# Attention output turned by 72-column groups and written transposed to DRAM, in a fused attention and MLP block

## The chip, the cores and the metric

The kernel runs on one core of one Trainium2 chip. The metric is the device time of one execution in microseconds, the median of three runs. The core has TensorE (PE, matrix products), VectorE (DVE), ScalarE (ACT), GpSimd (POOL) and the sync engine (SP). The last two issue DMA transfers here, SP plain ones and POOL those that accumulate. Each engine works through its own instructions in order.

## The reference

With x of 2048 tokens by 576 columns, normalised once to xn, the result is x plus an attention branch plus an MLP branch:

```python
def _A_ref(x, wqkv, wo):
    H = 32; Dh = D // H                      # 32 heads of 18 columns
    W, dil = 8, 2                            # 8 keys, every second token back
    q, k, v = split(x @ wqkv)
    idx = pos[:, None] - arange(W)[None, :] * dil
    attn = softmax(where(idx >= 0, q . k[idx] * Dh ** -0.5, -1e9))
    o = sum_w attn[w] * v[idx[w]]
    return o.reshape(B, S, D) @ wo

def _B_ref(x, w1, w2, w3, w4):
    h = gelu(layernorm(x) @ w1)              # four column blocks, then shifted by +1 -1 +2 -2 tokens
    x1 = x + shifted(h) @ w2
    return x1 + gelu(layernorm(x1) @ w3) @ w4    # 576 -> 4608 -> 576

xn = layernorm(x)
return x + _A_ref(xn, A_wqkv, A_wo) + _B_ref(xn, B_w1, B_w2, B_w3, B_w4)
```

Everything is fp32. The kernel multiplies in fp32r: each operand is split into a high and a low part (`split_w`, `signed`), and three of the four part products are summed.

## The kernel before

The work runs in stages, each ordered by hand. First q, k and v are computed and spilled to DRAM in 24 groups of 72 columns, four heads each (`qkvd`); then comes the token mixing with w1 and w2; then the MLP with w3 and w4. The MLP has two halves. For the first 6 pairs of column blocks it works in `units` of 512 tokens (`up`, L1241, and `down`). For the remaining 12 pairs it works in 24 steps, q = 0 to 23, twelve for each half of the tokens, with z = q - 24. One step is seven block products of a scheme that forms sums of operands in place of an eighth product (`product`, L1552, items P1 to P7) and eight down tiles (D0 to D7), in the order of `ORDER` (L1759). What else a step does hangs on these items: `at("D6", load_pair, ...)` places the load of a later pair of w3 blocks (L1382, L1385) after item D6, and so on. The last step, q = 23, is written out token by token in `ORDER_END` together with the output product o @ wo (items `k`, `y`, `c`: L2042, L2055, L2048) and the stores to `out`.

A down tile accumulates in PSUM (`down_mm`, L1288). `down_out` evicts it: into Y by ScalarE (L1300) or VectorE (L1303), or, for the ten tiles of `YD` whose rows live in DRAM, by ScalarE into a staging row (L1297), from which POOL adds it to `yd` by an accumulating DMA (L1298). `staging` (L1219) picks the row. While `EV[0]` is None these are three own rows of the pool `evp` and row 2 of Y in turn.

The attention is a generator (`attention`, L1100) that runs on VectorE beside TensorE's products. `bg` (L1197) is called between items with a budget in microseconds; each `yield` charges the estimated cost of the operation just issued. In a step the budget is 1.5 per item less what the item itself put on VectorE. For each of eight groups of four heads it computes eight pairs of multiply and reduce (w = 0 to 7, the last four as double width: L1162, L1165), a softmax, and in `av` (L1122) the weighted sum of the eight shifted v. A token is `p * 16 + j`: partition p holds 16 consecutive tokens. The result `o_` lies in `po[:, 0]`, 16 x 72 values on each partition, and one DMA writes it to `od`, in token order. The v of the next group is loaded right after. When z = -6 has come to item P4 the generator is run out whatever is left, its memory is given back, and rooms for wo, for the turned rows (`ST`) and for staging are taken from it.

The output product needs o with its columns on the partitions. In the steps z = -5 to -2 each item of a list reads one tile of 128 tokens of `od` in four DMAs (`load_o`, L1749), turns the tile before in blocks of 32 x 32 on VectorE (`o_turn`, L1757), and after every four tiles `put_o` writes the turned block in four DMAs to `on[b]` (576 x 512, L935). The end order then reads `on` into the operands of the output product (`read_x`, L1651, L1655). The loads of wo (`load_wo`, L1604, L1608) are placed in z = -5, those of w4 (L906) after D5 of each step.

Of the kernel before, what the change touches and what calls it, by code (L numbers as in the profile page):

```python
# [17 lines left out]
NT = S // 128  # L18
# [98 lines left out]


ORDER_END = """
xlp P1 cb gA lA D0 E0 P6 A0 P2 k2 P7 tf xr0.0 w40 gB wh24 P5 xr0.1 xr0.2 k3 xr0.3 xr0.4 xo1 xo3 D1  # L120
D2 E1 z3 P3 wt04 xr1.0 xr1.1 E2 A1 A2 D3 wh02 g22 lB E3 A3 D4 E4 D5 xh0.01 A4 D6 P4 wl wl02 wl24
z2 xs0.0 xs0.1 xs0.2 xt0.01 E5 A5 D7 E6 A6 w41 L3 xp1 xt0.13 xh1.01 l22 g12 E7 A7 xr1.2 xl1.01 l12
D8 xr1.3 xr1.4 E8 D9 xh0.13 gC lC rows xs0.3 E9 xt0.35 L2 xh0.57 xt0.57 A8 D10 E10 A9 D11 E11 L1
A10 D12 xl0.13 E12 A11 D13 xh1.13 A12 E13 xt1.01 A13 xt1.13 D14 D15 xo2 xh0.35 xr2.0 xr2.1 xr2.2
xr2.3 xr2.4 E14 E15 A14 xl0.01 xl0.57 A15 out k0.1 c0 k1.1 c1 k0.2 xl0.35 xs1.0 xs1.1 xs1.2 xs1.3
xh1.35 k0.5 k1.5 y0.2 k2.1 c2 xl1.35 xp2 xt1.35 y0.5 k0.6 y0.6 xl1.13 xh1.57 xl1.57 xh2.01 y1.5
xt1.57 k1.6 y1.6 k0.3 y0.3 k0.7 y0.7 k1.2 y1.2 k1.3 y1.3 k1.7 y1.7 xt2.13 L7 xt2.01 xl2.01 xh2.13
k0.4 y0.4 k2.2 k1.4 k3.1 c3 xl2.13 L5 y1.4 xr3.0 xr3.1 xp3 k2.6 y2.2 xs2.0 k2.5 xr3.2 xr3.3 y2.6
xr3.4 xs2.1 xs2.2 xs2.3 xt2.35 k3.6 y3.6 xh2.35 y2.5 k2.7 y2.7 xt2.57 k3.5 y3.5 xl2.35 k4.1 c4
k3.7 L10 y3.7 xh2.57 L15 xl2.57 k2.4 y2.4 xt3.13 o4 k4.2 xh3.13 k3.2 y3.2 xt3.01 L9 xs3.0 k4.6  # L130
y4.6 k4.5 y4.5 xh3.01 xl3.01 k5.1 o2 c5 xs3.1 k4.7 y4.7 L11 xs3.2 k3.4 k4.4 y3.4 k5.2 xh3.35 xs3.3
y4.4 xt3.35 xt3.57 xh3.57 y4.2 o8 y5.2 o3 xl3.13 xl3.57 k6.1 L13 c6 k7.1 c7 k3.3 k5.6 y5.6 y3.3 o5
k2.3 y2.3 o6 k5.7 o7 k5.5 y5.5 k7.6 xl3.35 k6.2 o0 y5.7 k5.3 y7.6 y5.3 k5.4 y5.4 o11 o1 k4.3 y4.3
o10 y6.2 k6.6 y6.6 k6.5 y6.5 k7.2 y7.2 k6.7 y6.7 k7.5 y7.5 k6.3 y6.3 k7.3 o9 o13.0 k7.7 o14 y7.3
y7.7 o15 k6.4 y6.4 k7.4 y7.4 o12 o13.1
"""


# [5 lines left out]
def fused_block(ctx, tc, x, wqkv, wo, w1, w2, w3, w4, out):  # L144
# [36 lines left out]
    TS, XS = KV[0:96, 2:3], KV[0:96, 3:4]  # L181
    ST = None
    qkvd = dram.tile([24, HALO + S, GC], F32, name="qkvd")
    od = dram.tile([S, D], F32, name="od")
    w3t = dram.tile([NWP, 32, 384], F32, name="w3t")
    yd = {t: dram.tile([128, D], F32, name=f"yd{t}") for t in YD}
    xn = [dram.tile([D, 512], F32, name=f"xn{b}") for b in range(NB)]
# [912 lines left out]
    def attention(ap):  # L1100
# [21 lines left out]
        def av(g):  # L1122
            if g == NG - 1:
                exp_now()
            L, v = Ls[g], vs[g]
            o, out = (o_, po[:, 0, :]) if g < NG - 1 else (
                qs[g].rearrange("p j (h d) -> p (j h) d", d=HD), qs[g].rearrange("p j d -> p (j d)"))
            Lf = L.rearrange("p j h w -> p (j h) w")
            dve.tensor_reduce(den[g], Lf, axis=AX.X, op=ALU.add)
            dve.reciprocal(den[g], den[g])  # L1130
            yield 0.8
            dve.tensor_tensor(Lf, Lf, den[g][:, :, None].to_broadcast([128, TPP * GH, W]),
                              op=ALU.mult)
            yield 0.6
            for w in range(W):
                vv = v[:, DIL * w:DIL * w + TPP, :].rearrange("p j (h d) -> p (j h) d", d=HD)
                dst = prod if w else o
                dve.tensor_tensor(dst, vv, Lf[:, :, w:w + 1].to_broadcast([128, TPP * GH, HD]),  # L1138
                                  op=ALU.mult)
                yield 1.35  # L1140
                if w:
                    dve.tensor_tensor(o, o, dst, op=ALU.add)  # L1142
                    yield 1.35
            sp.dma_start(od.rearrange("(p j) d -> p j d", p=128)[:, :, g * GC:(g + 1) * GC],
                         out.rearrange("p (j c) -> p j c", c=GC))

        yield None
        qs[0], ks[0] = load("q", 0, 0, False, pool), load("k", 1, 0, True, pool)
# [2 lines left out]
        for g in range(NG + 1):  # L1151
            if g < NG:
                q, k = qs[g], ks[g]
                L = Ls[g] = ap.tile([128, TPP, GH, W], F32, name="L", bufs=2)
                Lf = L.rearrange("p j h w -> p (j h) w")
                Lw = Lf.rearrange("p x w -> p w x")
                qf = q.rearrange("p j d -> p (j d)")
                for w, n in ((0, 1), (1, 1), (2, 1), (3, 1), (4, 2), (6, 2)):
                    dst = po[:, 2 - n:2, :]
                    win = bass.AP(tensor=k.tensor, offset=k.offset + DIL * w * GC,  # L1160
                                  ap=[list(k.ap[0]), [DIL * GC, n], [1, TPP * GC]])
                    dve.tensor_tensor(dst, qf[:, None, :].to_broadcast([128, n, TPP * GC]), win,  # L1162
                                      op=ALU.mult)
                    yield 0.15 + 1.2 * n
                    dve.tensor_reduce(Lw[:, w:w + n, :],  # L1165
                                      dst.rearrange("p w (x d) -> p w x d", d=HD),
                                      axis=AX.X, op=ALU.add)
                    yield 0.15 + 1.2 * n
                if g + 1 < NG:
                    qs[g + 1], ks[g + 1] = load("q", 0, g + 1, False), load("k", 1, g + 1, True)  # L1170
                mx = den[g] = ap.tile([128, TPP * GH], F32, name="mx", bufs=2)
                dve.tensor_tensor(L, L, mask4, op=ALU.add)
                yield 0.6
                dve.tensor_reduce(mx, Lf, axis=AX.X, op=ALU.max)
                yield 0.6
                dve.tensor_tensor(Lf, Lf, mx[:, :, None].to_broadcast([128, TPP * GH, W]),
                                  op=ALU.subtract)
                yield 0.6
                exp_now()
                state["exp"] = lambda L=L: act.activation(L, L, AF.Exp, scale=float(HD) ** -0.5)  # L1180
                if g == NG - 1:
                    vs[g] = load("k", 2, g, True)
                if g == 0:
                    yield 4.0
            if g:
                yield from av(g - 1)
                if g < NG - 1:
                    vs[g] = load("v", 2, g, True)

    state = {"gen": None, "debt": 0.0, "exp": None, "done": False}  # L1190

# [19 lines left out]
    def temp(t, n=512):  # L1211
        return Y[:, t, :n]
# [6 lines left out]
    def staging():  # L1219
# [1 line left out]
        if EV[0] == "nt":  # L1221
            return ntpool.tile([128, D], F32, name=f"ev{evc[0] % 3}")
        if EV[0] is None:
            n = evc[0] % 4
            return evp.tile([128, D], F32, name=f"ev{n}") if n < 3 else temp(2, D)
        return temp(EV[0][evc[0] % len(EV[0])], D)
    hid = {}

# [353 lines left out]
        for t, parts in prev:  # L1582
            yield lambda t=t, parts=parts: down(t, parts)

    otile = {}
    OF = {"A11": (0, 0), "A12": (0, 1), "A22": (0, 2), "S2": (1, 0), "S3": (1, 1), "S4": (1, 2),
          "S1": (1, 3), "B11": 0, "B21": 1, "B22": 2, "T1": 3, "T3": 4, "T2": 5, "T4": 6}
    WF, XF = {}, {}
# [152 lines left out]
            return f["tail"][0:96, i, :]  # L1741
        return f["hi"][:, v - 3, i, :] if v > 2 else f["lo"][:, v - 1, i, :]

    def load_o(t):
        b, i = divmod(t, 4)
        otile[t] = temp(9 + t % 3, D)
        for q in range(4):
            r = 512 * b + 128 * q + 32 * i
            sp.dma_start(otile[t][32 * q:32 * q + 32], od[r:r + 32, :])  # L1749

    def put_o(b):
        for q in range(4):
            n_put(b, q, on)

    def o_turn(t):
        c = t % 4 * 32
        dve.transpose(ST[:, :, c:c + 32], otile[t].rearrange("p (j c) -> p j c", c=32))  # L1757

    ORDER = "P1 D0 P2 P6 D1 P5 D2 P7 D3 P4 D4 P3 D5 D6 D7"  # L1759
    ORDERS = {0: "P1 P2 D0 P6 P5 P7 D1 D2 P4 P3 D3",  # L1760
              NWP - 1: "P1 D0 P2 P6 P5 P7 D1 P4 P3 D2 D3 D4 D5 D6 D7",
# [2 lines left out]
    for q in range(NQ):  # L1764
# [93 lines left out]
                at("D6", load_pair, q + 2 + (q == NWP - 2))  # L1858
        else:
            break  # L1860
        if -5 <= z <= -2:
            for i, (it, nx) in enumerate((("P6", "P6"), ("D1", "D1"), ("P5", "P5"), ("P4", "P4"))):
                t = 4 * (z + 5) + i
                at(it, o_turn, t)
                if t + 3 < NT:
                    at(nx, load_o, t + 3)

        if z < -1 and q + 1 != NWP:
            at("D5" if q else "D3", load_w4, NPL + pair(q + 1), 0)
        if 0 < q < 9:  # L1870
            at("D6", sums, 1, q - 1)
        if 0 < q - sb * NWP <= 5:
            at("D7", load_xa, YD[5 - 5 * sb + q - sb * NWP - 1])
        if -5 <= z < -1:
            at("P4", put_o, z + 5)
        if z == -2:
            at("D7", load_w4, NPL + pair(q + 1), 1)
        if z == -5:
# [10 lines left out]
        for it in ORDERS.get(q, ORDER).split():  # L1889
# [39 lines left out]
                tiles[int(it[1])]()  # L1929
            for f in plan.get(it, ()):  # L1930
                f()
            if (z < -6 or z == -6 and EV[0]) and (q, it) != (NWP, "P6"):
                bg(1.5 - spent[0], it == "P6" and q != NWP - 1 or (q, it) == (NWP, "P3"))
                spent[0] = 0.0
                if (z, it) == (-6, "P4"):
                    while not state["done"]:
                        bg(1e9)
                    apc.__exit__(None, None, None)
                    wop = tc.tile_pool(name="wop", bufs=1, reuse_waits="tile")
                    wopool = wop.__enter__()  # L1940
                    room_wa()
                    opc = tc.tile_pool(name="op", bufs=1, reuse_waits="tile")
                    room(opc.__enter__())
                    evc_pool = tc.tile_pool(name="evp", bufs=1, reuse_waits="tile")
                    evp = evc_pool.__enter__()
                    EV[0] = None
                    for t in range(3):
                        load_o(t)
    END, last = {}, {}
    q, g = NQ - 1, NQ - 2  # L1950

# [3 lines left out]
    def open_last():  # L1955
        nonlocal xlp, xlpool
        evc_pool.__exit__(None, None, None)
        opc.__exit__(None, None, None)
        EV[0] = (9, 11, 10, 2)
        xlp = tc.tile_pool(name="xlp", bufs=1, reuse_waits="tile")  # L1960
        xlpool = xlp.__enter__()
# [167 lines left out]
```

## Time and profile before

| what | us |
|---|---|
| median of three runs | 1261.26 |
| lowest and highest run | 1258.53, 1264.15 |
| the profiled execution | 1262.52 |
| its span, first to last instruction | 1260.7 |
| TensorE, VectorE, ScalarE, GpSimd busy | 1237.5, 959.4, 776.4, 298.6 |

The mean granted clock of TensorE is 0.995 of full speed. In the profile's rows an engine's busy time and the number of its instructions stand together; "PEld" is TensorE's loading of stationary operands, which overlaps its products. A chain row gives its start, its length and what ran. A wait row names who waited for what: the total, the number of times, the longest. A group row ends with the idle time just before its instructions and what ended it. Lines marked L are those of the kernel printed above.

### The profile page before, as it was taken

To read this page: it belongs to the slowest core of one execution; us is meant where nothing else is said; L and a number is where in the kernel's file an instruction comes from. 1 tells how busy PE (TensorE), PEld (TensorE's weight loads), DVE (VectorE), ACT (ScalarE), POOL (GpSimd) and SP (SyncE) were. 2 spreads that over 40 slices of the span, in tenths; PEclk is the share of its full clock that TensorE was granted. 3 is DMA by queue.
4 is the path that set the end of the run, shared out by engine and by line. 5 is a ranking of instruction groups with operands and counts; after the bars stand their busy time and mean duration, and the time that the engine had idled before them with its cause. 6 is when DMAs were issued, how large, how long until landed. Compare 5 with 4: busy or idle time off the path is not lost.

```text
span 1260.7 us, 20054 instructions
## 1 busy us (share of the span) xinstructions
PE 1237.5 (98%) x7305; PEld 1137.3 (90%) x7305; DVE 959.4 (76%) x1244; ACT 776.4 (62%) x1264; POOL 298.6 (24%) x436
## 2 busy tenths in 40 slices
PE   9999999999999999999999999999999999998798
PEld 8999988999898999999899998999899999887798
DVE  8877546698388989996678898999999865354486
ACT  4555566356455545547778678676768667575661
POOL 4523000031321121112123223222222222221230
PEclk9999999999999999999999999999999999899899
DMA  8879795168888695868688987989866878998885
GB/s 234 203 182 222 161 245 166 38 178 230 225 195 201 159 193 114 197 150 222 126 189 178 214 205 154 212 177 243 188 151 120 186 148 196 211 195 173 181 214 186
DMA packets 221627, 231.97 MB, mean 184 GB/s; under 512 B 100072, under 2 KB 157800, under 8 KB 221400
## 3 DMA queue, kind: packets, MB, share of 16 engines
q1 hardware_dynamic: 187864, 162.72, 46.3%
q0 software_dynamic: 33664, 67.97, 33.4%
q8 instruction: 57, 0.93, 0.3%
q14 instruction: 42, 0.34, 0.1%
HBM read 131.58 MB, written 108.30 MB: 190 GB/s over the span
## 4 chain that ended last, share of the span: by engine, by line
PE 63%; DMA 5%; ACT 2%; DVE 2%; issue 1%; SPq 0%; ACTq 0%; DVEq 0%
PE ps L1288 31%; PE cc L1558 18%; PE p L1252 10%; DMA w3st<-in_B_w_dram 3%; PE ca L2042 2%; PE cc L2042 1%; DMA Y<-in_B_w_dram 1%; PE cb L2042 1%; DMA yd<-Y 1%; DVE w3st L1393 0%; DMA xt<-xn 0%; DVE xt L954 0%; ACT Y L1297 0%; ACT ev L1297 0%; SPq L1382 0%
## 5 line engine op out<-in xcount | busy, mean ns | idle before, releaser
L1288 PEld LDWEIGHTS ps<-w,c 128*128 128x128 f32 x3456 | 481.3, 190 | 26.7 <-ACT ev L1297 6.4
L1288 PE MATMUL ps<-w,c 128*128 128x288 f32 x3456 | 491.7, 298 | 10.1 <-ACT ev L1297 5.3
L1298 POOL DMA_DIRECT2D yd<-Y x159 | 144.3, 910 | 373.5 <-ACT Y L1297 318.2
L1243 DVE TENSOR_TENSOR c<-Y,c 128x512 fp32r<-128x512 f32 x144 | 98.6, 685 | 87.8 <-ACT Y L1232 83.0
L1297 ACT COPY Y<-ps 128x576 f32<-128x576 f32 x159 | 100.9, 635 | 72.0 <-PE ps L1288 59.8
L1558 PE MATMUL cc<-xt,w3s 128*128 128x512 f32 (+1 forms) x504 | 129.2, 397 | 6.6 <-DVE Y L1568 6.0
L1558 PEld LDWEIGHTS cc<-xt,w3s 128*128 128x128 f32 (+1 forms) x504 | 93.2, 190 | 24.9 <-DVE Y L1568 6.5
L1300 ACT COPY Y<-ps 128x576 f32<-128x576 f32 x89 | 56.9, 639 | 52.3 <-PE ps L1288 51.0
L1162 DVE TENSOR_TENSOR po<-q,k 128x1152 f32<-128x1152 f32 (+1 forms) x48 | 84.2, 1754 | 0.8
L1558 PE MATMUL cc<-xB,w3a 128*128 128x512 f32 (+1 forms) x336 | 84.7, 392 | 0.0
L1165 DVE TENSOR_REDUCE L<-po 128x64 f32<-128x1152 f32 (+1 forms) x48 | 84.0, 1751 | 0.8
L1231 ACT ACTIVATE c<-p 128x512 fp32r<-128x512 f32 x48 | 28.7, 598 | 88.7 <-PE p L1252 88.7
L1138 DVE TENSOR_TENSOR po<-v,L 128x1152 f32<-128x1152 f32 x56 | 75.4, 1354 | 0.9
L1558 PEld LDWEIGHTS cc<-xB,w3a 128*128 128x128 f32 (+1 forms) x336 | 60.5, 188 | 10.0
L436 PE MATMUL p<-wb,xt 128*128 128x432 f32 (+1 forms) x336 | 68.3, 362 | 0.2 <-ACT wb L325 0.2
L1142 DVE TENSOR_TENSOR po<-po 128x1152 f32<-128x1152 f32 x49 | 66.4, 1355 | 0.9
L436 PEld LDWEIGHTS p<-wb,xt 128*128 128x128 f32 (+1 forms) x336 | 62.5, 189 | 3.3 <-ACT wb L325 0.6
L1568 DVE TENSOR_TENSOR Y<-cc,Y 128x512 f32<-128x512 f32 x49 | 33.5, 684 | 39.1 <-ACT Y L1564 34.6
L200 POOL TENSOR_TENSOR rs<-rs,mhalf 128x1 f32<-128x1 f32 x32 | 22.6, 707 | 163.5 <-DVE mv L203 93.6
L1269 ACT COPY ps<-Y 128x576 f32<-128x576 f32 x89 | 57.5, 646 | 3.1 <-DVE Y L1303 1.2
L708 PE MATMUL ca<-wb,xt 128*128 128x432 f32 (+1 forms) x280 | 58.5, 360 | 0.0
L708 PEld LDWEIGHTS ca<-wb,xt 128*128 128x128 f32 (+1 forms) x280 | 52.6, 189 | 2.8 <-ACT keep L715 0.4
(349 smaller groups left out, 2244.0 us busy)
## 6 DMA issues: line engine op xcount, KB each, us to landing
yd<-Y POOLq DMA_DIRECT2D x161, 288.0 KB, 6.0
Y<-in_B_w_dram SPq DMA_DIRECT2D x29, 576.0 KB, 6.0
w3st<-in_B_w_dram SPq DMA_DIRECT2D x56, 256.0 KB, 8.4
qkvd<-stg SPq DMA_DIRECT2D x44, 216.0 KB, 3.3
yd<-ev POOLq DMA_DIRECT2D x21, 288.0 KB, 7.7
w3st<-in_B_w_dram SPq DMA_DIRECT2D x92, 64.0 KB, 7.6
Y<-in_A_x_dram SPq DMA_DIRECT2D x16, 288.0 KB, 4.2
xn<-st SPq DMA_DIRECT2D x16, 288.0 KB, 4.4
```

Source lines behind the costliest of these rows:

```text
L436: pe.matmul(ps[:, :QB], xo[:n, o + k, a, :], W[:n, w + k, v, :], start=i == 0, stop=i == len(PLAIN) - 1)
L708: pe.matmul(ps, form(g // 2, x, n, a), W[:n, OP[w], v, :], start=start and i == 0, stop=stop and i == len(HALVES) - 1, skip_group_check=True)
L1138: dve.tensor_tensor(dst, vv, Lf[:, :, w:w + 1].to_broadcast([128, TPP * GH, HD]), op=ALU.mult)
L1142: dve.tensor_tensor(o, o, dst, op=ALU.add)
L1162: dve.tensor_tensor(dst, qf[:, None, :].to_broadcast([128, n, TPP * GC]), win, op=ALU.mult)
L1165: dve.tensor_reduce(Lw[:, w:w + n, :], dst.rearrange("p w (x d) -> p w x d", d=HD), axis=AX.X, op=ALU.add)
L1243: dve.tensor_tensor(h[:, 1, :], g, h[:, 0, :].bitcast(F32), op=ALU.subtract)
L1252: pe.matmul(ps, W3[f][:, w, :], x1n[b][:, a, :], start=n == 0, stop=n == len(PAIRS) - 1)
L1288: pe.matmul(ps[:, k, :HF], h[:, col], w[:, p, k * HF:(k + 1) * HF], start=n == 0 and not seed, stop=n == len(seq) - 1, skip_group_check=True)
L1297: act.copy(e.rearrange("p (h c) -> p h c", h=2), ps[:, :, :HF])
L1298: pool.dma_start(yd[t], e, accum_op=ALU.add)
L1558: pe.matmul(ps, WX[w][:k, v, SLOT[w], :], area[sb][xk][:k, a, :], start=onto is None and i == 0, stop=last and i == len(HALVES) - 1, skip_ ...
```

## The change

`od` and the functions `load_o`, `o_turn` and `put_o` go, with the calls that placed them in z = -5 to -2. In place of the one write to `od`, `av` turns the group itself, in three windows of 32 columns that start 24 columns apart, into the memory of the group's v. Block b of 32 partitions then holds 24 columns of the window for 512 tokens, which are the tokens of `on[b]`; four DMAs of 24 rows write them. The last group uses `po` like the others.

```diff
-            o, out = (o_, po[:, 0, :]) if g < NG - 1 else (
-                qs[g].rearrange("p j (h d) -> p (j h) d", d=HD), qs[g].rearrange("p j d -> p (j d)"))
+            o = o_
...
-            sp.dma_start(od.rearrange("(p j) d -> p j d", p=128)[:, :, g * GC:(g + 1) * GC],
-                         out.rearrange("p (j c) -> p j c", c=GC))
+            turned = v.rearrange("p j c -> p (j c)")[:, :3 * 512].rearrange("p (b x) -> p b x", b=3)
+            for b in range(3):
+                win = bass.AP(tensor=po.tensor, offset=po.offset + 24 * b,
+                              ap=[list(po.ap[0]), [GC, TPP], [1, 32]])
+                dve.transpose(turned[:, b, :].rearrange("p (c j) -> p j c", j=TPP), win)
+                yield 0.7
+            for b in range(NB):
+                sp.dma_start(dram_ap(on[b], g * GC * 512, [[512, 24], [24 * 512, 3], [1, 512]]),
+                             turned[32 * b:32 * b + 24])
```

The load of v moves from the end of `av` into the pairs of the next group, after the third:

```diff
                     yield 0.15 + 1.2 * n
+                    if w == 2 and g > 1:
+                        vs[g - 1] = load("v", 2, g - 1, True)
...
                 yield from av(g - 1)
-                if g < NG - 1:
-                    vs[g] = load("v", 2, g, True)
```

The attention may run up to item D2 of z = -5 instead of P4 of z = -6; its memory is given back there, without a room for turned rows. Staging has five own rows in place of three and Y[2]:

```diff
-            n = evc[0] % 4
-            return evp.tile([128, D], F32, name=f"ev{n}") if n < 3 else temp(2, D)
+            return evp.tile([128, D], F32, name=f"ev{evc[0] % 5}")
...
-            if (z < -6 or z == -6 and EV[0]) and (q, it) != (NWP, "P6"):
-                bg(1.5 - spent[0], it == "P6" and q != NWP - 1 or (q, it) == (NWP, "P3"))
+            if (z < -5 or z == -5 and EV[0]) and (q, it) != (NWP, "P6"):
+                bg(1.5 - spent[0], it == "P6" and q != NWP - 1)
                 spent[0] = 0.0
-                if (z, it) == (-6, "P4"):
+                if (z, it) == (-5, "D2"):
```

`ORDER_END` holds nearly the same items in another order. Its first lines, before and after:

```diff
-xlp P1 cb gA lA D0 E0 P6 A0 P2 k2 P7 tf xr0.0 w40 gB wh24 P5 xr0.1 xr0.2 k3 xr0.3 xr0.4 xo1 xo3 D1
-D2 E1 z3 P3 wt04 xr1.0 xr1.1 E2 A1 A2 D3 wh02 g22 lB E3 A3 D4 E4 D5 xh0.01 A4 D6 P4 wl wl02 wl24
+xlp gA lA P1 cb D0 D1 E0 E1 P2 P6 w40 A0 A1 D2 k2 P7 wh02 P5 xo1 D3 tf k3 z3 xr0.0 w41 xr0.1 P3
+wh24 xr0.2 xr0.3 xr0.4 E2 xr1.0 xr1.1 g22 A2 wt04 l22 D4 E3 E4 A3 A4 xt0.01 D5 E5 z2 g12 D6 A5 D7
...
```

In it P, D and E are products, down tiles and their evictions, A opens the next bank, `w40` and `w41` split the last w4, `xr` reads `on`, `xh`, `xt`, `xl` and `xs` form the operands from it, and `wh`, `wt`, `wl` those from wo.

## What the change should do to the time

> **What bounds the kernel now.** I read the page first, then the busy time by stage, the chain of work that ended last, the sync engine's timeline, and what VectorE waited for.
>
> ```profile
> span 1260.7 us, 20054 instructions
> PE 1237.5 (98%) x7305; PEld 1137.3 (90%) x7305; DVE 959.4 (76%) x1244; ACT 776.4 (62%) x1264; POOL 298.6 (24%) x436
> ```
>
> TensorE is busy for all but 23.2 us, so an edit that takes nothing from TensorE can only win back idle or slowed TensorE time. Where that time lies is read by stage. One step of the second MLP half (seven products, eight down tiles) is one window below; I call the steps q0 to q23. The first window is a step in mid-run, the next four are q19 to q22 from first product to first product, then q23 with its downs (the written-out end order), then the output products.
>
> ```profile
> core 0: us, PE busy (x) PEld busy (x) DVE busy (x) ACT busy (x) POOL busy (x), PEclk, DMA share, GB/s
> 1003.50:1027.50 24.00, 24.00 (x147) 21.97 (x146) 22.33 (x23) 16.80 (x28) 7.05 (x9) 1.00 0.73 135
> 1048.40:1072.40 24.00, 24.00 (x146) 21.98 (x146) 12.44 (x17) 16.80 (x27) 5.99 (x8) 1.00 0.98 233
> 1072.40:1102.20 29.80, 26.90 (x146) 24.53 (x146) 12.02 (x17) 16.83 (x27) 6.10 (x8) 0.89 0.91 213
> 1102.20:1129.20 27.00, 24.58 (x146) 21.86 (x146) 12.17 (x18) 18.06 (x29) 7.09 (x9) 1.00 0.91 194
> 1129.20:1157.20 28.00, 24.78 (x146) 21.74 (x145) 16.13 (x23) 16.79 (x29) 5.99 (x7) 1.00 0.84 176
> 1157.20:1204.80 47.60, 40.32 (x244) 37.08 (x243) 20.11 (x28) 29.63 (x46) 13.90 (x17) 0.93 0.88 183
> 1204.80:1257.00 52.20, 52.17 (x393) 51.93 (x391) 43.44 (x91) 19.06 (x34) 9.75 (x13) 1.00 0.73 204
> ```
>
> A step at full pace takes 24.0 us. q20, q21 and q22 take 29.8, 27.0 and 28.0: 5.8 + 3.0 + 4.0 = 12.8 us lost. The chain has the price of one product and of three downs:
>
> ```profile
> 1067.60 4.79 PE ps L1288 x36
> 1072.39 1.61 PE cc L1558 x7
> ...
> 1081.29 11.22 DMA w3st<-in_B_w_dram
> ...
> 1092.59 0.60 ACT w3a L1398
> ...
> 1093.93 0.53 ACT ev L1297
> ...
> 1094.51 7.68 PE ps L1288 x36
> ...
> 1111.96 8.56 DMA w3st<-in_B_w_dram
> ...
> 1137.53 11.12 DMA w3st<-in_B_w_dram
> ...
> 1157.49 14.81 DMA Y<-in_B_w_dram
> ```
>
> So q23 with seven products and sixteen downs needs 7 x 1.61 + 16 x 1.60 = 36.9 us and took 47.6: 10.7 lost. The output products lose nothing (52.17 busy of 52.2). All told 12.8 + 10.7 = 23.5 us are lost after 1072, and next to nothing before. The chain also says how: a load of w3 (`w3st`) arrives late, ScalarE's cast L1398 waits for it, the eviction L1297 stands behind that cast in ScalarE's order, and TensorE waits for the bank. In q23 it is the load of w4 into Y.
>
> Why do these loads come late? The sync engine issues them in program order:
>
> ```profile
> 1024.51 1.02 SPq L1382 DMA_DIRECT2D w3st<-in_B_w_dram  x2
> ...
> 1080.36 1.47 SPq L1382 DMA_DIRECT2D w3st<-in_B_w_dram  x2
> ...
> 1109.61 3.03 SPq L1382 DMA_DIRECT2D w3st<-in_B_w_dram  x2
> ...
> 1134.76 4.80 SPq L1382 DMA_DIRECT2D w3st<-in_B_w_dram  x2
> ```
>
> In mid-run the issue falls at the first product of the step (1024.4). In q20, q21, q22 it falls 8.0, 7.4 and 5.5 us after it (1072.4, 1102.2, 1129.2). What stands ahead on that queue, and on VectorE, is the late work on o:
>
> ```profile
> SPq L1749 <- DMA yd<-Y: 9.1, 2, 6.5
> SPq L1749 <- DMA od<-q: 7.5, 1, 7.5
> ...
> L1757 DVE STREAM_TRANSPOSE st<-Y 128x576 f32<-128x576 f32 x16 | 11.9, 763 | 27.6 <-DMA Y<-in_B_w_dram 9.7 <-DMA on<-st 8.5 <-DMA wr<-in_A_wo_dram 7.7
> ...
> Y<-od SPq DMA_DIRECT2D x64, 72.0 KB, 3.2
> on<-st SPq DMA_DIRECT2D x16, 288.0 KB, 8.1
> ```
>
> 64 reads and 16 writes stand in one queue with the weight loads, each with waits of its own; the sixteen turns held VectorE idle for 27.6 us; and the DMA share is 0.98, 0.91 and 0.91 where mid-run has 0.73.
>
> **The change, part by part.**
>
> *The late reads, turns and writes go.* 64 x 72 KB and 16 x 288 KB are 9.2 MB, with their SP issues and 16 x 0.763 = 12 us of VectorE. With the queue clear, the w3 issue goes back to the start of the step. In mid-run a w3 load has from 1024.4 to its cast 13.3 us into a step (q19: cast at 1061.72, step from 1048.40):
>
> ```profile
> 1061.72 0.84 ACT L1398 CAST w3a<-w3st 128x768 fp32r<-128x768 f32 x1
> w3st<-in_B_w_dram SPq DMA_DIRECT2D x56, 256.0 KB, 8.4
> ```
>
> 8.4 us to landing leaves some 4 us of slack, and even the 11.2 us of q20 would fit. I take back 12.3 of the 12.8 us of q20 to q22; 0.5 stays for the six loads of wo, which remain in q19.
>
> *The end.* In q23 the w4 load was issued at 1157.49, because VectorE's previous w4 split was late behind the turns, and it took 14.81 us among the last writes of o, the first reads of them, and accumulates.
>
> ```profile
> 1176.76 3.36 PE L1558 MATMUL cc<-xt,w3s 128*128 128x512 f32 x7 [5.72 <-DVE Y L1568]
> 1180.12 7.45 PE ps L1288 x48
> ```
>
> This cost TensorE 5.72 us of idle, then a product of 3.36 us for 1.61 and four downs of 7.45 for 6.39 (the clock granted is 0.93 in this window): 5.7 + 1.8 + 1.1 = 8.6 us. Mid-run issues the same load ahead of the step's first product, so I count it gone. The other 2.1 stays, and I charge 2.1 more because q23 compressed to 37 us must still read the new forms' inputs (0.88 x 47.6 = 42 us of DMA work in the window, of which the writes of o, 1.2 of 183 GB/s x 47.6 us = 8.7 MB, go). Net gain at the end: 6.5 us. The end order is rearranged, with the same kinds of work; by itself I cost that at nothing, below 2 us either way. Two output rows stand last on the queue as before.
>
> *The turns move into the attention.* 24 of 128x512 instead of 16 of 128x576: by elements 512/576 x 763 = 0.68 us each, 16.3 us in all. They lie beside TensorE's products, paid from the attention's budget of VectorE time, as the 0.7 in the code says. What is unproven is their write, whose elements lie 64 bytes apart; all rows of transposes here write runs of 32. From below: 0.68 us, nothing lost. From above the dearest element that VectorE shows is the reciprocal's, 553/64 = 8.6 ns, so 4.4 us a turn.
>
> ```profile
> L1130 DVE RECIPROCAL mx<-mx 128x64 f32<-128x64 f32 x8 | 4.4, 553 | 0.3
> 420.00:567.00 147.00, 147.00 (x874) 133.93 (x873) 139.89 (x122) 75.52 (x123) 25.15 (x29) 1.00 0.74 153
> 640.00:960.00 320.00, 319.22 (x1922) 291.35 (x1921) 288.47 (x305) 233.16 (x366) 86.27 (x101) 1.00 0.85 191
> ```
>
> VectorE has 7.1 us free from 420 to 567 (three groups, nine turns) and 31.5 from 640 to 960 (the five other groups, fifteen turns). I take 0.7 us, the nearest row being the same instruction. The Trainium skill, "SBUF — State Buffer", section "Door 1: The DMA port swizzle", speaks against it: accesses that leave a 16-byte line pay a penalty, and here every written element does. It gives no size, and no run here shows one; at twice the time, an estimate, the sum stays, because the extra still fits the free time above.
>
> *The attention ends later.* Its last stretch:
>
> ```profile
> 984.25 0.68 DVE L1129 TENSOR_REDUCE mx<-L 128x64 f32<-128x512 f32 x1
> L1142 DVE TENSOR_TENSOR q<-q,po x7: 1347/1354/1360, 989.5 to 1025.0; 128x1152 f32<-128x1152 f32 x7
> ```
>
> By the yields in the code these 42 us held 21.65 us of budget, 0.51 a us. The 24 x 0.7 = 16.8 more take 33 us: the end moves from 1026 to 1059, just where the new closing point lies (q19, before its third down: 1048.4 + 6 x 1.6 = 1058 to 1060). VectorE had 11.6 us free in q19 (12.44 busy of 24). At most a few operations are forced there; cost 0, and up to 10 us if I am wrong (a rival).
>
> *The stores.* Per group four DMAs of 24 rows in runs of 2 KB replace one with runs of 288 bytes, the same 590 KB with the padding left out. The v load moves behind the third pair of the next group and waits for them. In a tight group that place and the start of the weighting are
>
> ```profile
> 512.00 1.36 DVE L1162 TENSOR_TENSOR po<-q,k 128x1152 f32<-128x1152 f32 x1
> 529.78 0.68 DVE L1129 TENSOR_REDUCE mx<-L 128x64 f32<-128x512 f32 x1
> v<-qkvd SPq DMA_DIRECT2D x6, 576.0 KB, 9.3
> ```
>
> 18 us for 9.3, cost 0, with at most 3 us per group if SP is held. On SP, weight loads would stand behind that wait; 4 us of slack covers it.
>
> *Staging.* Five own rows replace three and Y[2] in q19 to q22. Evictions wait less for a free row, never longer: nothing on the low side, and on the high side only what these steps lose, which the 12.3 already counts. I add 0.
>
> **Sum.** 12.3 + 6.5 = 18.8 us: span 1241.9. The profiled execution took 1262.52 us, 1.8 more than its span; the median of the runs is 1261.26, so the time is 1261.26 - 18.8 = 1242.5.
>
> **Rivals.**
> 1. *The end stays bound by its loads.* For it: a DMA share of 0.88 there and ScalarE's in-order casts. Against: 1.2 MB of writes less and w4 issued earlier. q20 to q22 alone give 12.3: 1249.0.
> 2. *The attention closes late* and a burst of forced VectorE work, followed by wo loads waiting for its memory on SP, holds q19 and q20. For it: a 33 us estimate that lands on the closing point. Against: free VectorE time. It gives back 10 us: 1252.5.
> 3. *Nothing moves.* The loads are late because DMA is full, not because of SP's order. For it: 0.98 share in q19. Against: q19 lost nothing at that share. About 1260.
> 4. *Slower: the turns' scattered writes.* At a price t per turn, 24 x (t - 0.7) less the 38.6 us free falls on TensorE through VectorE's order; it eats the gain from t = 3.1 us, four and a half times the plain turn. At 4.4 us it costs 50 us: 1292. Against: strided operands elsewhere (the products with L) run at the plain rate. The skill's rule above is this rival's ground, without a size.
>
> **How the numbers follow.** Forecast 0.60, rival 1 0.23, rival 2 0.07, rival 3 0.06, rival 4 0.04. This kernel's measurement can tell about 0.5%, 6.3 us, from no change. Faster: 0.60 + 0.23 + 0.06 of rival 2 = 0.89; same: 0.01 + 0.06 = 0.07; slower: 0.04. The range runs from all 23.5 us won back (1237.8, rounded to 1237.0) to rival 2 (1253.0).
>
> **What would show it.** Right: windows of 24.0 us for q20 to q22; the w3 issue at the first product; no wait for a w3 or w4 load ahead of an eviction; transposes of 0.7 us at eight places between 440 and 1060; the output products starting near 1186. Wrong: transposes over 1.4 us; products waiting for VectorE between 420 and 570; a stall in q19 or q20 behind the wo loads; TensorE idle by more than 4 us in q23.

## The result, and the profile after

| | before | after |
|---|---|---|
| median of the runs, us | 1262.68 | 1242.37 |
| lowest and highest run, us | 1258.53, 1264.15 | 1240.77, 1245.73 |
| the profiled execution, us | 1262.52 | 1240.77 |
| its span, us | 1260.7 | 1239.0 |

The ratio is 0.9848, with an interval of 0.9815 to 0.9881. (Before was run once more beside after, which moves its median from 1261.26 to 1262.68.) The profiled execution of after is the fastest of its four, so the spans differ by 21.7 us and the medians by 20.3. The first lines of the page after:

```profile
span 1239.0 us, 19946 instructions
PE 1230.8 (99%) x7305; PEld 1133.3 (91%) x7305; DVE 972.0 (78%) x1252; ACT 776.5 (63%) x1264; POOL 299.4 (24%) x436
```

TensorE has the same 7305 products in 6.7 us less busy time, and its idle time went from 23.2 to 8.2 us. 6.7 + 15.0 = 21.7: two thirds of the gain are waits that went, one third is products that had run slowly in the windows that held those waits.

The windows by stage of after: q19 to q22 and then the start of the end order, each cut at 24 us, so that kernels can be compared line by line. "PEclk" is the last column but two, then come DMA share and GB/s.

```profile
core 0: us, PE busy (x) PEld busy (x) DVE busy (x) ACT busy (x) POOL busy (x), PEclk, DMA share, GB/s
1048.00:1072.00 24.00, 24.00 (x147) 21.97 (x146) 16.60 (x20) 16.80 (x28) 6.00 (x8) 1.00 0.86 201
1072.00:1096.00 24.00, 24.00 (x147) 21.96 (x146) 9.66 (x13) 16.80 (x28) 5.98 (x8) 1.00 0.74 153
1096.00:1120.00 24.00, 24.00 (x147) 21.97 (x146) 11.32 (x15) 19.31 (x32) 7.65 (x10) 1.00 0.66 125
1120.00:1144.00 24.00, 24.00 (x147) 21.97 (x146) 13.30 (x17) 16.79 (x28) 5.92 (x8) 1.00 0.64 126
1144.00:1183.00 39.00, 38.90 (x257) 36.63 (x256) 22.12 (x32) 30.02 (x47) 15.15 (x18) 1.00 0.99 207
```

TensorE is busy for all but 0.1 us, at full clock. In the experiments I use two measures. One is the number of products in the last four windows: 147 + 147 + 147 + 257 = 698 here. The other is the delay of a product: e1, with the old end order, apart, the kernels derived from after run the same products in the same order, so I take the product that after starts at 1183, how much later another kernel starts it, and subtract the same delay at 1048. That gives the microseconds lost in between.

The sync engine's timeline of after, in q19 and later (start, length, queue, line, tile, number of DMAs):

```profile
1057.67 3.34 SPq L1149 DMA_DIRECT2D on<-k  x4
1064.02 1.16 SPq L1607 DMA_DIRECT2D wr<-in_A_wo_dram  x2
1069.39 0.37 SPq L905 DMA_DIRECT2D Y<-in_B_w_dram  x1
...
1074.47 0.99 SPq L1386 DMA_DIRECT2D w3st<-in_B_w_dram  x2
...
1098.24 0.90 SPq L1386 DMA_DIRECT2D w3st<-in_B_w_dram  x2
...
1120.15 0.99 SPq L1386 DMA_DIRECT2D w3st<-in_B_w_dram  x2
...
1142.08 0.38 SPq L905 DMA_DIRECT2D Y<-in_B_w_dram  x1
```

The w3 loads of q20, q21 and q22 are issued within 2.5 us of the first product of their step, where before it was 8.0, 7.4 and 5.5. The w4 load is issued at 1142.08, 2 us ahead of q23; before it was 1157.49, at q23's first product. The first store of the last group stands at 1057.67: the attention ends there.

The first output product of after, the only output product that waits, and the turns of the first seven groups (timeline and groups; the bracket is the idle time before it and who ended it):

```profile
1181.21 0.29 PE L2016 MATMUL cc<-wfs,xfh 128*128 128x288 f32 x1
1206.05 0.40 PE L2016 MATMUL cc<-wfs,c 96*128 96x288 f32 x1 [1.55 <-DMA c<-wr]
...
L1146 DVE STREAM_TRANSPOSE v<-po 128x512 f32<-128x512 f32 x21 | 21.0, 1064 | 0.2
```

q23 starts at 1144.2, so it takes 37.0 us, the full-pace price. A turn takes 1.06 us. The turn of 576 columns in before takes 0.763, which scales to 0.68 for 512.

### The profile page after: what moved, and what is told of

The parts are those of the page before. It is cut to its first block, busy times and chain, and to the rows that moved or that the text cites. A ratio compares the mean times of both kernels' runs of the same rounds, so it can differ in the third digit from the quotient of the medians.

```text
span 1239.0 us, 19946 instructions
## 1 busy us (share of the span) xinstructions
PE 1230.8 (99%) x7305; PEld 1133.3 (91%) x7305; DVE 972.0 (78%) x1252; ACT 776.5 (63%) x1264; POOL 299.4 (24%) x436
## 4 chain that ended last, share of the span: by engine, by line
PE 64%; DMA 3%; DVE 2%; ACT 2%; issue 2%; SPq 0%; DVEq 0%; ACTq 0%; POOLq 0%
PE ps L1292 32%; PE cc L1562 20%; PE p L1256 10%; DMA w3st<-in_B_w_dram 1%; PE ca L2016 1%; DMA c<-on 1%; PE cc L2016 1%; DMA c<-wr 1%; DMA w3a<-wr 0%; DVE wr L1674 0%; DVE w3st L1397 0%; PE cb L2016 0%; DVE w L915 0%; DVE po L1167 0%; DVE w3s L1408 0%
## 5 line engine op out<-in xcount | busy, mean ns | idle before, releaser
L1140 DVE TENSOR_TENSOR po<-po 128x1152 f32<-128x1152 f32 x56 | 75.9, 1355 | 1.0
```

## The experiments

Four reasons stood against each other. **Q**: the late work on o holds the queues of SP and VectorE, and the weight loads behind it come late. **B**: its bytes fill the DMA engines. **O**: the new end order does a good part. **W**: it takes the writes to do the damage. Each kernel ran four to ten times. Small losses are read from the windows and not from medians, because the stretch before q19 varies from profile to profile: among e1, e3 to e6, e9 and e10, which do not touch it, the product that after starts at 1048 comes from 0.9 us earlier to 4.2 us later.

**1. The end order alone.** After with the old `ORDER_END`, and before with the new one:

```diff
 # after, e1_old_end_order             # before, e2_new_end_order_before
-    ORDER_END = """xlp gA lA P1 ...    -    ORDER_END = """xlp P1 cb gA ...
+    ORDER_END = """xlp P1 cb gA ...    +    ORDER_END = """xlp gA lA P1 ...
```

> The changed kernel with the end order of before, nothing else. Theory Q (the late reads, turns and writes of o held SP's order, VectorE's order and the DMA engines, and so made the weight loads late): q20 to q22 stay at 24.0 us each and q23 takes 37 to 41 us, time 1240 to 1248. Rival O (the rearranged end order won q23's 10.7 us): q23 takes 45 us or more, time 1250 to 1254.

> The kernel before with the new end order, nothing else. Theory Q: q20 to q22 lose 12 to 13 us as before, q23 still takes 44 us or more, time 1257 to 1264. Rival O: q20 to q22 lose 12 to 13 us, q23 takes 37 to 40, time 1250 to 1254.

1242.32 us (ratio to before 0.9841, 0.9821 to 0.9860) and 1267.45 us (1.0032, 1.0017 to 1.0047). e1 loses nothing in q20 to q22. Its last window, in the columns used above:

```profile
1144.00:1183.00 39.00, 38.08 (x251) 35.80 (x250) 19.10 (x27) 29.54 (x47) 13.98 (x17) 1.00 0.91 196
```

The chain of work of e2:

```profile
1079.93 11.46 DMA w3st<-in_B_w_dram
...
1155.07 15.76 DMA Y<-in_B_w_dram
```

The old order runs 251 products in the last window where the new one runs 257, about a microsecond, and gives it back by the end. With the late work in place the new order wins nothing: the same loads are late. e2's median is even 4.4 us above that of before run beside it (1263.02), clear of the noise and above my range of 1257 to 1264. Its profiled execution, the fastest of its ten, has a span within 0.2 us of before's and does not show where these 4 us go; that stays open. O falls.

**2. The late work, one kind at a time.** Into after I put back, in z = -5 to -2 and at the old places, work that nothing uses: the reads (52 DMAs of 72 KB from `on` into free rows of Y), or the writes (16 DMAs of 288 KB, in runs of 512 bytes, to a spare tensor).

```diff
+    def late_read(t):                                   # e3_late_reads
+        b, i = divmod(t, 4)
+        for q in range(4):
+            sp.dma_start(temp(9 + t % 3, D)[32 * q:32 * q + 32],
+                         dram_ap(on[b], 128 * 512 * q + 18432 * i, [[D, 32], [1, D]]))
```
```diff
+    def late_write(b):                                  # e4_late_writes
+        for q in range(4):
+            src = temp(9, D)[32 * q:32 * q + 32]
...
+            sp.dma_start(dram_ap(late[b], 128 * q, [[512, 32], [32 * 512, 18], [1, 128]]), blk)
...
+        if -5 <= z < -1:
+            at("P4", late_write, z + 5)
```

> The changed kernel with 52 reads of 72 KB from the finished o into the free rows 9 to 11 of Y put back in q19 to q22, at the places of before, with nobody using what they read; no turns, no writes. Theory Q, in the form that the waits behind the turns did the harm: 0 to 3 us lost in q20 to q22, time 1242 to 1246. Rival B (the bytes alone, whoever waits): 3.7 of the 8.5 MB, so 4 to 9 us lost, time 1246 to 1252.

> The changed kernel with 16 writes of 288 KB in runs of 512 bytes to a spare tensor put back after P4 of q19 to q22; no reads, no turns. Theory Q, in the form that the waits behind the turns did the harm: 0 to 3 us lost in q20 to q22, time 1242 to 1246. Rival B: 4.7 of the 8.5 MB in the shortest runs, so 5 to 9 us lost, time 1247 to 1252.

1244.92 us (0.9865, 0.9837 to 0.9892) and 1244.54 us (0.9857, 0.9838 to 0.9876). The window of e3 with the highest DMA share:

```profile
1072.00:1096.00 24.00, 24.00 (x147) 21.96 (x146) 9.64 (x14) 16.79 (x28) 6.01 (x7) 1.00 1.03 253
```

Step windows of e4:

```profile
1072.00:1096.00 24.00, 24.00 (x147) 21.94 (x145) 7.66 (x13) 15.12 (x25) 5.04 (x6) 1.00 0.99 233
1096.00:1120.00 24.00, 23.23 (x139) 20.97 (x138) 11.61 (x16) 19.85 (x33) 7.60 (x9) 1.00 0.98 206
```

DMA engines busy for the whole window (1.03, 0.99, 0.98), and TensorE loses nothing to the reads and 0.9 us to the writes. A full DMA share is no sign of a loss by itself: B, as a matter of the share, falls.

**3. Two and three kinds together.** e5 adds turns to the reads, e6 all three, e9 reads and writes without turns, e10 turns and writes without reads. These have a room `ST` for the turned rows and before's staging (three own rows and Y[2]).

```diff
+    def late_turn(t):
+        c = t % 4 * 32
+        dve.transpose(ST[:, :, c:c + 32], temp(9 + t % 3, D).rearrange("p (j c) -> p j c", c=32))
...
+        if -5 <= z <= -2:
+            for i, (it, nx) in enumerate((("P6", "P6"), ("D1", "D1"), ("P5", "P5"), ("P4", "P4"))):
...
+                at(it, late_turn, t)                    # e5, e6, e10
...
+                    at(nx, late_read, t + 3)            # e5, e6, e9
...
+            at("P4", late_write, z + 5)                 # e6, e9, e10
```

> The changed kernel with 52 late reads of 72 KB and 13 late turns of what they read, at the places of before (from the last item but four of q19 on), into a spare block; staging of three own rows and Y[2]; no late writes. A read must now wait on SP until VectorE has turned the row it overwrites, and VectorE's queue waits for the read. Theory Q: the ring of waits between SP and VectorE is what makes the weight loads late, so q20 to q22 lose 4 to 10 us and q23 1 to 6, time 1247 to 1256. Rival W (only all three together, through the writes that hold the turns): 0 to 3 us lost, time 1242 to 1246.

> As the run with late reads and turns, and the 16 late writes of 288 KB of the turned block to a spare tensor as well: the late work of before in full for q20 to q22, beside the new attention. Theory Q and rival W: q20 to q22 lose 10 to 13 us and q23 6 to 11, w3 issues 5 to 8 us after the first product, time 1256 to 1265. Rival N (the gain has another source, the attention's new close, staging or memory): under 5 us lost in all, time below 1248.

> As the run with all three, without the 13 late turns: 52 reads of 72 KB and 16 writes of 288 KB of a constant block, so that nobody waits for a turn. Theory B (bytes: by the windows of before, q20 holds 0.91 x 29.8 = 27 us of DMA work for a step of 24, and q23 42 for 37, so the weight loads are late whoever waits): q20 to q22 lose 8 us or more, time 1252 or more. Theory Q (the ring of waits between VectorE's turns and SP): 0 to 4 us lost, time 1241 to 1247.

> As the run with all three, without the 52 late reads: 13 turns of whatever lies in the rows and 16 writes of the block, each turn waiting for the writes of the block before. Theory B: 4.7 MB of writes alone fit, as they did by themselves: 0 to 4 us lost, time 1241 to 1247. Theory Q, if the wait of a turn for the writes is the harmful one: 5 us or more lost, time 1248 or more.

| kernel | median, us | ratio to before | products missing by 1183 | us lost, 1048 to 1183 |
|---|---|---|---|---|
| e3 reads | 1244.92 | 0.9837 to 0.9892 | none | 0 |
| e4 writes | 1244.54 | 0.9838 to 0.9876 | 7 | 0.9 |
| e5 reads, turns | 1243.14 | 0.9828 to 0.9869 | none | 0 |
| e9 reads, writes | 1259.86 | 0.9965 to 1.0005 | 117 | 16.3 |
| e10 turns, writes | 1264.76 | 0.9997 to 1.0034 | 138 | 19.6 |
| e6 all three | 1268.70 | 1.0042 to 1.0095 | 182 | 26.5 |

One step window each of e5, e6, e9 and e10, in this order:

```profile
1072.00:1096.00 24.00, 24.00 (x147) 21.96 (x146) 12.71 (x19) 16.79 (x29) 5.99 (x8) 1.00 1.03 256
```
```profile
1072.00:1096.00 24.00, 19.66 (x112) 17.42 (x111) 6.04 (x9) 10.08 (x18) 3.12 (x4) 0.97 0.93 223
```
```profile
1072.00:1096.00 24.00, 20.70 (x120) 18.32 (x120) 3.92 (x7) 10.98 (x19) 3.69 (x5) 1.00 0.98 237
```
```profile
1120.00:1144.00 24.00, 21.82 (x129) 19.14 (x128) 15.49 (x21) 16.61 (x27) 5.96 (x7) 1.00 0.84 160
```

e6 brings the whole loss back and 3 us more (26.5 against the 23.5 of before; its median lies above my range of 1256 to 1265), so the late work on o accounts for all that the change won. Neither turns nor reads are needed for a loss of 16 us and more, but the writes are, together with one of the other two. W was right in e5, but it asked for all three, and e9 and e10 refute that. For e9 B had the better forecast, for e10 Q; neither had both. How the writes do it stands in the sync engine's timeline. First e3, reads alone:

```profile
1064.54 6.86 SPq L1750 DMA_DIRECT2D Y<-on  x12
...
1074.63 0.50 SPq L905 DMA_DIRECT2D Y<-in_B_w_dram  x1
...
1077.25 0.99 SPq L1386 DMA_DIRECT2D w3st<-in_B_w_dram  x2
```

The same stretch of e9, reads and writes:

```profile
1061.96 6.81 SPq L1752 DMA_DIRECT2D Y<-on  x12
1068.81 0.42 SPq L1609 DMA_DIRECT2D wr<-in_A_wo_dram  x1
1069.35 1.78 SPq L1752 DMA_DIRECT2D Y<-on  x4
1071.24 5.25 SPq L935 DMA_DIRECT2D late<-st  x4
1076.53 2.56 SPq L1609 DMA_DIRECT2D wr<-in_A_wo_dram  x1
1079.20 2.54 SPq L906 DMA_DIRECT2D Y<-in_B_w_dram  x1
1081.78 1.42 SPq L1613 DMA_DIRECT2D wr<-in_A_wo_dram  x1
1083.36 1.01 SPq L1388 DMA_DIRECT2D w3st<-in_B_w_dram  x2
```

From 1061.96 to the w3 load at 1083.36 SP is issuing almost without a gap. The four writes take 5.25 us to issue, and the single loads behind them lengthen: the w4 load of this step takes 2.54 us to issue where it took 0.37 in after and 0.50 in e3. I summed the issues from 1060 to 1140, 80 us, without the pauses between them that a row of several DMAs includes. Issuing takes 13.8 us in after, 33.9 in e4, 38.2 in e3 and 38.9 in e5, which lose little or nothing, and 59.5 in before, 63.2 in e6 and 64.5 in e9, which lose much. In these three SP issues for 74 to 81% of the time, and the w3 loads, last in its order, come late: 1082.31, 1109.79 and 1136.08 in e6 against 1074.47, 1098.24 and 1120.15 in after. That these issues lie on the path, and not beside it, the chain of work of e6 shows. It goes through the writes (L935), the load of wo (L1609) and the load of w4 (L906) into the w3 load:

```profile
1073.55 1.98 SPq L935
...
1075.57 3.58 SPq L1609
...
1079.25 1.99 SPq L906
...
1082.76 10.10 DMA w3st<-in_B_w_dram
```

The delays of the steps' first products show where the time goes. In q20 to q22 e9 loses 12.7 us, e6 14.6 and e10 7.8, and behind them 3.6, 11.9 and 11.8. So e10 goes another way. SP issues for only 39.7 us there, and its DMA share (0.91, 0.88 and 0.84 in the three windows from 1072 to 1144) is below that of e4 (0.99, 0.98 and 0.79) in the first two. The chain of work of e10 in q20:

```profile
1073.55 8.15 DMA w3s<-w3st
1082.24 10.63 DMA w3st<-in_B_w_dram
```

The next w3 load waits until POOL's accumulate has read its staging memory (`w3s<-w3st`). From issue to landing that takes a median of 7.6 us in e10 between 1050 and 1160, against 3.7 in after, 4.6 in e4, 3.9 in e5, 5.3 in e9 and 4.0 in e6 (four or five transfers each); and then the load itself takes over 10. What e10 loses behind q22 hangs on the load of w4 for q23. Two rows of its sync engine's timeline, then what SP and ScalarE waited for:

```profile
1152.52 3.76 SPq L935 DMA_DIRECT2D late<-st  x4
1156.37 2.14 SPq L906 DMA_DIRECT2D Y<-in_B_w_dram  x1
...
SPq L935 <- DVE st L1757: 33.1, 4, 14.0
...
ACT w L913 <- DMA Y<-in_B_w_dram: 11.2, 1, 11.2
```

The same two rows of e9, which has no turns:

```profile
1149.05 4.00 SPq L935 DMA_DIRECT2D late<-st  x4
...
1156.50 0.39 SPq L906 DMA_DIRECT2D Y<-in_B_w_dram  x1
```

In e10 the last writes wait for their turn and so come directly ahead of the w4 load, which takes 2.14 us to issue and for which ScalarE's split then waits 11.2 us. In e9 the writes come 3.5 us earlier, the load takes 0.39 us to issue, and the split waits 2.6. e6 and before have the turns and go as e10 does: the writes at 1154.28 and 1153.72, the load at 1159.06 and 1157.49, and 10.0 and 8.7 us of waiting.

So the loss has at least two paths: in q20 to q22 w3 loads that a busy SP issues late (e9, e6, before) or that come late through the accumulates (e10), and in q23 a w4 load close behind writes that waited for their turn (e10, e6, before). The writes are in both. Both accounts were made after the runs, and no kernel was made to test them. What in the writes lengthens the issues and landings of other transfers stays open.

**4. The price of the turns.** Each turn three times, and twice:

```diff
-                dve.transpose(turned[:, b, :].rearrange("p (c j) -> p j c", j=TPP), win)
+                for _ in range(3):                      # 2 in e11_turns_twice
+                    dve.transpose(turned[:, b, :].rearrange("p (c j) -> p j c", j=TPP), win)
```

> The changed kernel with each of the 24 turns in the attention issued three times, without more budget: 48 x 1.06 = 51 us more on VectorE. The prediction's price of a slow turn (each turn at 3.2 us; free VectorE time 420 to 567 about 5 us against 19 more, 640 to 960 about 30 against 32 more): TensorE loses 12 to 18 us, time 1254 to 1261. Rival (VectorE's lag is taken up by slack between the hidden tiles and the products that need them): under 4 us lost, time 1242 to 1247.

> The changed kernel with each turn in the attention issued twice, without more budget: 24 x 1.06 = 25 us more on VectorE. Pooled price (the prediction's: only what does not fit into the free time of a whole stage is lost, 5 us from 420 to 567 and 30 from 640 to 960): 0 to 5 us lost, time 1241 to 1248. Burst price (three times cost 38 us for 51: each group's three turns come in one run, and what they exceed a local slack falls on TensorE, about 1.6 us a group): 8 x (3.2 - 1.6) = 13 us lost, time 1252 to 1258.

1280.53 us (1.0142, 1.0120 to 1.0165) and 1257.29 us (0.9968, 0.9950 to 0.9986): 48 x 1.06 = 51 us more of VectorE cost 38 us, and 25 us cost 15. TensorE's longest wait in e7:

```profile
PE cc L1563 <- DVE Y L1573: 11.6, 3, 4.8
```

The free time of VectorE is not one pool. Three turns of a group come one behind the other, with VectorE's evictions of products and down tiles behind them, so a group pays for what its own few microseconds cannot take, whatever is free later. The delay of the same products shows it: it grows in steps at the groups' turns and stays level between them, by 6.5, 0, 7.6, 7.6, 4.1, 5.1, 7.1 and 0.8 us at the eight groups of e7, and by 0.7, 0, 2.1, 2.1, 2.1, 4.4, 4.9 and 0 in e11. The price by bursts, fitted to e7, forecast 13 for e11 and 15 came; it is right for the sum, but its 1.6 us of slack is a mean over very unequal groups. The pooled price missed both times.

**5. Turns written in whole runs.** The same turns with the written elements next to each other:

```diff
-                dve.transpose(turned[:, b, :].rearrange("p (c j) -> p j c", j=TPP), win)
+                dve.transpose(turned[:, b, :].rearrange("p (j c) -> p j c", c=32), win)
```

> The changed kernel with the turns written in runs of 32 elements, as all turns of before; the columns of o then stand in another order, so the attention's part of the output is not the reference's. The turn takes about 0.70 us instead of 1.06, 8.5 us less on VectorE. If the scattered write costs only VectorE time that is covered: time within 2 us of 1242. If it is on the path as the burst price has it: up to 3 us faster, 1239 to 1241.

1244.45 us (0.9875, 0.9853 to 0.9896). The instruction view of these turns, minimum, median and maximum in ns:

```profile
L1146 DVE STREAM_TRANSPOSE v<-po x21: 669/702/714, 446.0 to 1012.6; 128x512 f32<-128x512 f32 x21
```

The same view of after has a median of 1056 ns, so the scattered write costs half as much again. The kernel is no faster without it, so its 24 x 0.35 = 8.5 us are covered.

**6. The v load in its old place.**

```diff
-                    if w == 2 and g > 1:
-                        vs[g - 1] = load("v", 2, g - 1, True)
...
                 yield from av(g - 1)
+                if g < NG - 1:
+                    vs[g] = load("v", 2, g, True)
```

> The changed kernel with the load of v back at the end of av, where SP must wait for the four stores of the turned group to land before it issues the load and whatever stands behind it. If the move of the load matters: a held SP makes weight loads late by up to 6 us in the groups that end near an issue, 2 to 8 us lost, time 1244 to 1251. If it does not: within 2 us of 1242.

1246.81 us (0.9884, 0.9858 to 0.9909), 4.4 more than after. Two windows of e8, in which after has 62.87 and 63.00 us busy:

```profile
567.00:630.00 63.00, 60.68 (x354) 54.55 (x353) 40.82 (x50) 45.36 (x71) 13.36 (x16) 1.00 0.85 197
945.00:1008.00 63.00, 61.03 (x370) 55.40 (x369) 54.41 (x59) 47.32 (x75) 18.87 (x22) 1.00 0.71 148
```

The sync engine's waits of e8:

```profile
SPq L1114 <- DMA on<-v: 25.2, 7, 8.7
```

The load of v overwrites the turned rows and holds SP until their stores have landed, with other loads behind it: 25.2 us in all, against 12.2 in after. In the first window the chain of work goes from this wait into the load of a product's operand:

```profile
567.27 3.54 DMA on<-v
...
571.95 12.23 DMA xB<-xn
```

In the second it is a weight load: the w3 load is issued at 934.71, behind the load of v, where in after it stands ahead of it at 929.01. Moving the load of v is worth about 4 us of the change, 2.2 and 2.0 in these two windows.

## Why the prediction came out right, and where it was off

*12.3 of the 12.8 us of q20 to q22.* Right: 12.8 came, and the w3 issue went to the start of the step, so rival 3 falls. The half microsecond for the wo loads was not needed.

*Why they were lost.* I named 64 reads and 16 writes with waits of their own, the turns and the DMA share. e6 shows that these together are the cause. e3 and e5 show that the reads, even with the turns, do no harm, and that a share of 1.03 does none. So "each with waits of its own" was the weak part: the four writes of a block do it, with either partner, and in q20 to q22 of before, e6 and e9 much of it is SP's time to issue and not a wait. In q23 it is a wait, that of the last writes for their turn. I had not weighed these two rows of the sync engine's timeline of before, the writes and the w4 load behind them:

```profile
1068.51 4.66 SPq L935 DMA_DIRECT2D on<-st  x4
...
1075.74 2.29 SPq L906 DMA_DIRECT2D Y<-in_B_w_dram  x1
```

*6.5 us of 10.7 at the end.* The load was the right one, and the turns have to do with it, since e9 without them loses 3.6 us here where e6 and e10 lose 11.8 and more. But I had them delay its issue through VectorE's split. e9 issues it no earlier (1156.50), and what the turns delay is the writes directly ahead of it. The size was off too. All 10.7 came back, so rival 1 falls. The 2.1 that I let stay were part of the late load's train, and the 2.1 charged for compressed reads did not appear in q23, at a DMA share of 0.99. One price did appear later: the wait of 1.55 us at 1206.05 for POOL's accumulating DMA that builds a part of wo's operand in `c` (`c<-wr`). So the sum of the trace is 12.8 + 10.7 - 1.6 = 21.9, and 21.7 was measured between spans, against 18.8 predicted. That the median lies at 1242.37, next to 1242.5, is in part luck, since the gain between spans was 2.9 us more than I summed: after's profiled execution is 1.6 us below its median, and I subtracted from a median of before that came out 1.4 higher when a run was added.

*The end order at 0.* Right (e1, e2); inside the bound of 2 for after.

*The turns at 0.7 us, covered.* The duration was wrong: 1.06. The rule of the Trainium skill, "SBUF — State Buffer", section "Door 1: The DMA port swizzle", that an access which leaves a 16-byte line pays a penalty, agrees with the trace. The size is 1.5 here: e12 takes the scatter away and finds 0.70. That the line is the reason no run shows. That it is covered was right (e12). Rival 4's break-even of 3.1 us was wrong, because it pooled the free time: between e11 (2.13 us a turn, 0.9968) and e7 (3.2 us, 1.0142) the line to 1 is crossed at about 2.3 us.

*The attention's end at 1059, on the closing point.* Right: the last store is issued from 1057.67, q19 is at full pace and the wo loads start at 1064.02. Rival 2's burst did not come.

*Stores and v load at 0.* Right for the change as made. e8 says what the move was needed for, which I had not priced.

*Staging at 0.* e5 runs with three rows and Y[2] and loses nothing in these windows; with the writes it was not tried apart from a partner. e4 had five own rows and wrote from rows of Y, the kernels with two or three kinds had the old staging and wrote from a room, so part of the step from e4 to e9 could be staging. The waits speak against it: from 1060 to 1183 ScalarE's evictions into staging rows wait for nothing but TensorE in e6, e9 and e10 (3.0 us in all on the rows `ev` in each, 3.6 in after). No run takes the two apart. Why an issue behind the writes takes 2.3 us instead of 0.4 is left open too.

## What to carry to other kernels

A queue that carries weight loads has a budget of issuing time like any engine: sum the lengths of its issues over a step. Where they filled three quarters of the time (59.5 us and more of 80 here), what stood last was late; at half of it (38.9 and less) it was not. A low sum is no proof, since e10 lost 20 us at 39.7, and a full DMA share alone says little. Work moved onto an engine with free time is paid at the place where it bursts, not from the sum of what is free. An edit that reuses memory must look at who loads into it next and on which queue that load waits.

## What was not expected of the hardware

- The length of an SP issue varies by a factor of six to seven: the same w4 load took 0.37 us in after, and 2.29 in before and 2.54 in e9 behind writes in 512-byte runs.
- The DMA share stood at 1.03 over a whole step (253 to 256 GB/s in e3 and e5), with no loss on TensorE, while e10 lost 20 us with shares of 0.91 and less after 1072.
- One third of the span's gain, 6.7 of 21.7 us, is the same products running shorter. The granted clock was 0.89 and 0.93 in the two windows of before that lost most, and 1.00 in all windows of after.
- A 32 x 32 turn of 128x512 fp32 takes 1056 ns (median) when the elements that it writes lie 64 bytes apart, and 702 when they lie side by side.
